# Fused attention and MLP on one core: the packed values computed with e1 stationary in 128x32 tiles, divided at once, and turned by two transposes

## Chip, cores and metric

The kernel runs on one core of a Trainium2 chip. The metric is the time of one execution on the device in microseconds (us); the number given for a kernel is the median of its runs.

## The reference

For each of 8 batches and 8 heads there are queries, keys and values of 576 rows by 64 columns, and 32 packed queries `p`. The attention is done twice: `p` attends to the keys and values, which gives 32 packed rows per head, and then the queries attend to those packed rows. The heads side by side give 4608 tokens of 512 columns, which go through a two-layer MLP.

```python
p_packed = sm_attn(p, k, v)            # softmax(p k^T / 8) v : 32 x 64 per head
out = sm_attn(q, p_packed, p_packed)   # softmax(q p_packed^T / 8) p_packed : 576 x 64 per head
x = out.transpose(0, 2, 1, 3).reshape(8 * 576, 512)
h = x @ w_in                           # 512 -> 2048
g = s * relu(h) ** 2 + b
y = g @ w_out                          # 2048 -> 512
```

## The kernel before

**Layout.** A batch is worked on as a whole. Heads are numbered `head(a, g) = 2g + a`, with `a` in 0..1 and `g` in 0..3, so that 4 groups of 32 packed rows fill 128 partitions for each `a`. The 576 rows of keys and values are taken in `NC = 6` chunks of `R = 96`.

**Stages of a batch.** Each has a letter in the order of work.

- `Tk`, `Tq` (`on_pe`, batches 0 and 1) or `Dk`, `Dq` (`on_dma`, later ones) turn keys and queries; `L..` are loads on the POOL queue; `V` (`order_v`) copies the loaded values, `vn`, into `vr`, ordered by chunk and head.
- `F` (`first_scores`) makes the scores of `p` against the keys, for one `a` at a time, and ScalarE writes their exponentials to `e1` (named `e` in the profile): 96 partitions, and for each `a`, chunk `c` and `g` 32 columns.
- `P` (`packed`) makes the packed values without their division. The stationary operand is `vr` of two heads (96x128), the moving one is `e1` of both `a` (64 columns); 6 chunks are summed for each of 4 head pairs, half of the pairs in `P.0` and half in `P.1`. Six more matmuls for each half, with `e1` stationary and a column of ones (`ones1`) moving, give the sums of the softmax. So a batch has 24 matmuls of 64 columns and 12 of one column in `pps`. The reciprocals of the sums go to `rd`, and with the scale to `rs`. The packed values are copied, undivided, to `ppd`, once in place and once to the other 64 partitions (`(c2, d)` on partitions, since the second scores want them in both halves): VectorE and ScalarE do two copies each.
- `S` (`second_scores`) makes the scores of the queries against `ppd` in 64x32 tiles of the array; their exponentials, with `rs` as a scale by pointer for each partition, are `e2` (also `e` in the profile). `A` (`weights`, for batch 0 `weights_half`) sums them with a block matrix of ones and divides: `aT`.
- `W` (`packed_w`) multiplies `ppd` by `w_in`, two chunks of 512 columns at a time, in 64x32 tiles; `scaled` copies the result to `pw` with `rd` as a scale, one half on ScalarE and one on VectorE.
- `M` (`mlp_in`, for batch 0 partly `mlp_in_half`, `h`) multiplies `pw` by `aT`: 4 matmuls of 288 columns into `hps`, a relu to `rlu`, a square to `gT`.
- `O` (`Out.step`) is the second layer: `Ob.txn` is `n` of the 16 matmuls of 512 columns that a block `t` of 128 tokens needs in `yps`; behind the sixteenth, VectorE writes `ysb` with the bias and the SP queue stores it.

`BT` (`bias_sums`) and `BC` (`bias_rows`) work out the bias once, from all of `w_out`, in batch 1's part; `BT` uses 128x32 tiles. `Z` and `Y` are matmuls of zeros that keep TensorE busy in the first microseconds.

**Order.** Nothing is scheduled at run time. Every instruction is pinned to the program's order on its engine (the helpers on lines 62, 65 and 73, which is why nearly all rows of the profile carry those lines), and the program's order is a list of words written out by hand:

```python
        O1.0x4 O1.1x2 P2.0 O1.1x1 P2.1 O1.1x5 W2.0 O1.1x6 S2 O1.1x2 O1.2x3 A2.0 O1.2x2 A2.1 O1.2x9 V3
```

So the `O` matmuls of one batch are the filling between the steps of the next one's attention, and the number behind an `x` is the time, in matmuls, that a step's followers have.

**PSUM.** `psh` has two buffers of two banks each, for all that is called `hps`; `psy` has four of one bank, for `yps`, `pps` and the like. The raw loads `kn`, `qn`, `vn` have one buffer each, and so have `vr`, `e1` and `e2`; `ppd`, `kT` and `qT` have two, by the batch's parity.

Of the kernel before, what the change touches and what calls it, by code (L numbers as in the profile page):

```python
# [14 lines left out]
def kernel(  # L15
# [18 lines left out]
    P = 128  # L34
# [68 lines left out]
    ones1 = constp.tile([P, 1], BF16, name="ones1")  # L103
# [45 lines left out]
    vr, e1, e2, rd, rs, aT, pw, pps, s2 = {}, {}, {}, {}, {}, {}, {}, {}, {}  # L149
# [38 lines left out]
    def on_pe(b, what, half):  # L188
# [5 lines left out]
        split = b == 0 and what == "q" and half == 1  # L194
# [24 lines left out]
    def order_v(b, h0=0, h1=H):  # L219
        if h0 == 0:  # L220
            vr[b] = attp.tile([R, NC, H, D], BF16, tag="vr", name="vr")
        vec.tensor_copy(
            out=vr[b][:, :, h0:h1, :].rearrange("r c h d -> r h c d"),
            in_=raw["v", b][:, h0:h1, :].rearrange("r h (c d) -> r h c d", c=NC),
        )
# [25 lines left out]
    def packed(b, half):  # L251

        if half == 0 or b == 0:
            pps[b] = psy.tile([P, NB], F32, tag="y", name="pps")
        pp = pps[b]
        for hp in range(2 * half, 2 * half + 2):
            for c in range(NC):
                mm(
                    pp[:, hp * 2 * NP:(hp + 1) * 2 * NP],
                    vr[b][:, c, 2 * hp:2 * hp + 2, :],  # L260
                    e1[b][:, :, c, hp, :],
                    start=(c == 0),
                    stop=(c == NC - 1),
                )
        a = half
        sums = pp[:, HP * 2 * NP:HP * 2 * NP + 2]
        for c in range(NC):
            mm(
                sums[:, a:a + 1],
                e1[b][:, a, c, :, :],  # L270
                ones1[0:R, :],
                start=(c == 0),
                stop=(c == NC - 1),
            )
        pd = ppd[b % 2]
        src = pp[:, 0:HP * 2 * NP].rearrange("p (g a j) -> p a g j", g=HP, a=2)
        if half == 0:
            rd[b] = smp.tile([P, 2], F32, tag="rd", name="rd")
            rs[b] = smp.tile([P, 2], F32, tag="rs", name="rs")
        if b == 0:  # L280
            vec.reciprocal(out=rd[b][:, a:a + 1], in_=sums[:, a:a + 1])
            gs = slice(2 * half, 2 * half + 2)
            for a in range(2):
                for to in (D * a, D - D * a):
                    (act.copy if half else vec.tensor_copy)(
                        out=pd[to:to + D, a, gs], in_=src[D * a:D * a + D, a, gs]
                    )
        elif half == 0:
            return
        else:  # L290
            vec.reciprocal(out=rd[b][:], in_=sums)
            for a in range(2):
                vec.tensor_copy(out=pd[D * a:D * a + D, a], in_=src[D * a:D * a + D, a])
                act.copy(out=pd[D - D * a:2 * D - D * a, a], in_=src[D * a:D * a + D, a])
        if half == 1:
            vec.tensor_scalar_mul(out=rs[b][:], in0=rd[b][:], scalar1=scale)

    def second_scores(b, by_half=False, with_w=False):
# [21 lines left out]
        for a in range(2):  # L320
            act.activation(
                out=e2[b][:, a, :].rearrange("p (i s) -> p i s", i=2),
                in_=tiles[a][:, :, 0:HS],
                func=AF.Exp,
                scale=rs[b][:, a:a + 1],
            )

    def exp_half(b, tiles, a, hf):
# [4 lines left out]
            scale=rs[b][:, a:a + 1],  # L333
        )

    def weights_half(b, hf):
# [3 lines left out]
        cols = slice(hf * HS, (hf + 1) * HS)  # L340
        for a in range(2):
            mm(dps[:, a, 0:HS], onesbd[:], e2[b][:, a, cols], start=True, stop=True)
        if hf == 0:
            exp_half(b, s2[b], 0, 1)
        ld = smp.tile([P, 2, HS], F32, tag="ld", name="ld")
        act.activation(out=ld[:], in_=dps[:, :, 0:HS], func=AF.Ln)
        rcd = smp.tile([P, 2, HS], F32, tag="rcd", name="rcd")
        act.activation(out=rcd[:], in_=ld[:], func=AF.Exp, scale=-1.0)
        if hf == 0:
            exp_half(b, s2[b], 1, 1)  # L350
        vec.tensor_tensor(out=aT[b][:, :, cols], in0=e2[b][:, :, cols], in1=rcd[:], op=ALU.mult)

    def weights(b, a):
# [7 lines left out]
        rcd = smp.tile([P, S], F32, tag="rcd", name="rcd")  # L361
        act.activation(out=rcd[:], in_=ld[:].rearrange("p a s -> p (a s)"), func=AF.Exp, scale=-1.0)
        vec.tensor_tensor(out=aT[b][:, a, :], in0=e2[b][:, a, :], in1=rcd[:], op=ALU.mult)

    def packed_w(b, chs):
# [20 lines left out]
        if len(chs) > 1:  # L386
            for a in range(2):
                dst = pw[b][:, a, chs[0] * NB:(chs[0] + 2) * NB].rearrange("p (i f) -> p i f", f=NB)
                scaled(b, a, dst, pair[a][:], a == 0)
        if len(chs) != 2:  # L390
            ch = chs[-1]
            for a in range(2):
                scaled(b, a, pw[b][:, a, ch * NB:(ch + 1) * NB], single[a][:], a == 0 and ch > 0)

    def scaled(b, a, out, in_, on_act):
        if on_act:
            act.activation(out=out, in_=in_, func=AF.Copy, scale=rd[b][:, a:a + 1])
        else:
            vec.tensor_scalar_mul(out=out, in0=in_, scalar1=rd[b][:, a:a + 1])
# [168 lines left out]
    def run(word):  # L568
# [35 lines left out]
        elif what == "P":  # L604
            packed(*n)
# [41 lines left out]
    vec.memset(ones1[:], 1.0)  # L647
# [69 lines left out]
```

## Time and profile before

| | |
|---|---|
| median of 3 runs | 253.81 us (253.78 to 254.29) |
| the profiled execution | 253.64 us, of which its span is 251.9 us |
| granted TensorE clock | 1.00 |
| TensorE busy | 243.2 us, 97% of the span |
| VectorE, ScalarE busy | 145.1 and 145.7 us, 58% each |
| largest groups on TensorE | 592 `yps` matmuls, 145.2 us; 512 `hps<-aT,pw`, 75.4 us |
| loads and stores | 35.48 MB in DMA packets, mean 141 GB/s |

The span runs from the first to the last instruction that the profiler saw on the core; the time of an execution is a little longer. A listed matmul length is the latency of one; matmuls overlap, so a group's busy time is less than count times length. A line of the timeline gives the start of a group, the time from its first start to its last end, its engine, its operands (out<-in), its tile (rows*columns of the array) and shape, its count, and in brackets the idle time of the engine before it and what ended it. `PEld` is the loading of stationary operands, which overlaps the matmuls.

### The profile page before, as it was taken

What the parts mean: (1) busy time and instruction counts of PE and PEld (TensorE: products, weight loads), DVE (VectorE), ACT (ScalarE), POOL (GpSimd) and SP (SyncE); (2) the same over time, 40 slices, a digit from 0 to 9 for tenths busy, and PEclk for the clock granted to TensorE, in tenths of its full rate; (3) what the DMA queues carried; (4) which work ended last, traced back from release to release, by engine and by line L of the source; (5) the groups of instructions that cost most, each with busy time, mean ns of one, the idle gap of its engine ahead of it and who ended that gap; (6) DMA issues with size and microseconds to landing.
All of it is one profiled execution on the core that took longest, in us unless ns stands there. A gap on an engine that the chain in (4) does not pass through costs nothing.

```text
span 251.9 us, 5279 instructions
## 1 busy us (share of the span) xinstructions
PE 243.2 (97%) x2178; PEld 136.8 (54%) x2178; DVE 145.1 (58%) x279; ACT 145.7 (58%) x235; POOL 29.1 (12%) x43
## 2 busy tenths in 40 slices
PE   7988899999999999999999999999999999999994
PEld 2554466356644664466546664466545665456553
DVE  4438767598547664476358544756364662664531
ACT  2357654668756854868387565567336785465400
POOL 8633212000300030000300030003000000000000
PEclk9999999999999999999999999999999999999999
DMA  6999999999795969439694979587987711120042
GB/s 73 179 206 207 203 203 200 201 193 185 131 221 126 180 110 214 96 83 186 113 216 86 187 128 217 108 158 132 216 176 138 140 37 46 52 75 1 3 125 85
DMA packets 59449, 35.48 MB, mean 141 GB/s; under 512 B 32160, under 2 KB 54944, under 8 KB 59424
## 3 DMA queue, kind: packets, MB, share of 16 engines
q0 software_dynamic: 25184, 18.61, 49.7%
q1 hardware_dynamic: 34192, 16.49, 29.4%
q8 instruction: 17, 0.28, 0.4%
q14 instruction: 8, 0.07, 0.1%
q10 hardware_dynamic: 48, 0.03, 0.0%
HBM read 37.23 MB, written 9.44 MB: 185 GB/s over the span
## 4 chain that ended last, share of the span: by engine, by line
PE 86%; DMA 10%; POOL 1%; issue 1%; DVE 0%; ACT 0%; POOLq 0%
PE yps L62 50%; PE hps L62 32%; DMA w_out_sb<-in_moe_w_out_dram 7%; DMA vn<-in_v_dram 3%; PE pps L62 3%; PE hps L65 1%; POOL kn L73 1%; POOL pn L73 0%; PE pps L65 0%; POOL vn L73 0%; DVE ysb L73 0%; ACT pbd L73 0%; POOL identb L73 0%; POOLq L73 0%; POOLq L701 0%
## 5 line engine op out<-in xcount | busy, mean ns | idle before, releaser
L62 PE MATMUL yps<-w_out_sb,gT 128*128 128x512 bf16 (+1 forms) x592 | 145.2, 374 | 0.7 <-DMA w_out_sb<-in_moe_w_out_dram 0.7
L73 ACT ACTIVATE rlu<-hps 128x576 bf16<-128x576 f32 x124 | 74.9, 648 | 35.2 <-PE hps L62 34.9
L62 PEld LDWEIGHTS <-gT 128*128 128x128 bf16 x592 | 54.6, 98 | 50.9 <-issue 7.4
L73 DVE TENSOR_TENSOR gT<-rlu 128x576 bf16<-128x576 bf16 x128 | 58.1, 458 | 33.1 <-ACT rlu L73 28.7
L62 PE MATMUL hps<-aT,pw 128*128 128x288 bf16 x512 | 75.4, 285 | 0.9 <-DVE pw L73 0.9
L62 PEld LDWEIGHTS <-pw 128*128 128x128 bf16 x512 | 49.5, 97 | 28.0 <-DVE pw L73 1.5
L73 DVE SCALAR_TENSOR_TENSOR ysb<-yps,svec,biasrep 128x512 f32<-128x512 f32 (+1 forms) x37 | 27.0, 733 | 21.6 <-PE yps L62 21.6
L73 DVE TENSOR_TENSOR aT<-e,rcd 128x576 bf16<-128x576 bf16 x16 | 12.1, 757 | 21.6 <-ACT rcd L73 21.5
L73 POOL DMA_DIRECT2D kn<-in_k_dram x9 | 6.9, 768 | 130.4 <-DMA kT<-kn 99.2
L73 ACT ACTIVATE pw<-hps,rd 128x1024 bf16<-128x1024 f32 x14 | 15.6, 1114 | 10.6 <-PE hps L62 10.4
L73 DVE TENSOR_SCALAR pw<-hps,rd 128x1024 bf16<-128x1024 f32 x14 | 17.9, 1280 | 3.9 <-PE hps L62 3.8
L73 ACT ACTIVATE e<-hps 96x768 bf16<-96x768 f32 x16 | 12.1, 803 | 8.2 <-PE hps L62 8.2
L73 ACT ACTIVATE e<-hps,rs 128x576 bf16<-128x576 f32 (+1 forms) x18 | 11.4, 684 | 6.4 <-PE hps L62 6.3
L73 ACT CAST ppd<-pps 64x128 bf16<-64x128 f32 (+1 forms) x18 | 4.5, 248 | 18.1 <-DVE ppd L73 16.1
L62 PE MATMUL zps<-zb 128*128 128x512 bf16 x42 | 12.1, 424 | 1.2 <-DVE zb L73 1.2
L73 ACT ACTIVATE ld<-hps 128x576 f32<-128x576 f32 x16 | 10.3, 645 | 3.2 <-PE hps L62 2.5
L62 PEld LDWEIGHTS <-ppd 64*32 64x32 bf16 x384 | 5.0, 89 | 11.7 <-issue 10.2
L73 ACT ACTIVATE rcd<-ld 128x576 f32<-128x576 f32 x16 | 10.9, 683 | 0.5
L62 PE MATMUL hps<-w_in_sb,ppd 64*32 64x512 bf16 x224 | 9.8, 381 | 0.0
L62 PEld LDWEIGHTS <-vr 96*128 96x128 bf16 x192 | 7.6, 97 | 3.2 <-issue 1.4
L73 DVE COPY vr<-vn 96x3072 bf16<-96x3072 bf16 (+1 forms) x9 | 7.7, 861 | 1.3 <-DMA vn<-in_v_dram 1.2
L62 PE MATMUL pps<-e,vr 96*128 96x64 bf16 x192 | 8.2, 192 | 0.2 <-ACT e L73 0.2
(60 smaller groups left out, 115.4 us busy)
## 6 DMA issues: line engine op xcount, KB each, us to landing
out_dram<-ysb SPq DMA_DIRECT2D x23, 192.0 KB, 2.4
kn<-in_k_dram POOLq DMA_DIRECT2D x7, 576.0 KB, 7.2
qn<-in_q_dram POOLq DMA_DIRECT2D x7, 576.0 KB, 12.4
vn<-in_v_dram POOLq DMA_DIRECT2D x7, 576.0 KB, 9.8
out_dram<-ysb SPq DMA_DIRECT2D x24, 128.0 KB, 2.4
w_in_sb<-in_moe_w_in_dram POOLq DMA_DIRECT2D x4, 512.0 KB, 13.3
w_out_sb<-in_moe_w_out_dram POOLq DMA_DIRECT2D x4, 512.0 KB, 18.5
out_dram<-ysb SPq DMA_DIRECT2D x23, 64.0 KB, 2.1
```

What stands on the lines that cost most here:

```text
L62: return tc.keep_in_program_order(nc.tensor.matmul(*a, **kw))
L65: return tc.keep_in_program_order(nc.tensor.transpose(*a, **kw))
L73: return lambda *a, **kw: tc.keep_in_program_order(f(*a, **kw))
```

## The change

`packed` swaps the operands. `e1` of one `a`, one chunk and one `g` (96x32) is stationary, at column tile `g` of the array, and `vr` of that head with a column of ones behind it (65 columns) is moving. A batch has 48 such matmuls, four tiles in turn, all of `a = 0` first; partitions of `pps` are now `(g, j)`, and column 64 holds the softmax sum of each partition. `vr` becomes one fixed tile, 66 columns a head, whose last two are set to 1.0 once. Behind the matmuls, VectorE takes the reciprocal of the sums and writes the divided values, twice side by side, to `pk`. A new step `X` (`turned`) transposes `pk` in two 128x128 transposes into the other half of `pps`' bank, and one VectorE copy of 256 columns fills `ppd`. Since `ppd` is now divided, `rs` is gone (the scale of the second exponentials is a constant) and `scaled` becomes `evict`, a copy without a scale.

For batch 0, `P` stays in two halves. Both halves of its `q` are split between ScalarE and VectorE, its second exponentials are all issued ahead of the logarithm, the product for `aT` becomes a word of its own (`G`, `weigh_half`), and the first chunk of `pw` is copied on VectorE in two halves of 256 columns (`first_w`, the second one at the word `E`). The list of words is written anew, with one `P` for each batch from 1 on, an `X` some five `O` behind it, and `O`, `M` and `W` in other places. The loads keep their order on the POOL queue. On the SP queue two stores stand ahead of one pair of `Dq`, `Dk` in place of behind it. Behind `BT` there are 544 `O` matmuls in place of 545.

```diff
-    ones1 = constp.tile([P, 1], BF16, name="ones1")
+    DV = D + 2
+    vr = constp.tile([R, NC, H, DV], BF16, name="vr")
...
-        split = b == 0 and what == "q" and half == 1
+        split = b == 0 and what == "q"
...
     def order_v(b, h0=0, h1=H):
-        if h0 == 0:
-            vr[b] = attp.tile([R, NC, H, D], BF16, tag="vr", name="vr")
         vec.tensor_copy(
-            out=vr[b][:, :, h0:h1, :].rearrange("r c h d -> r h c d"),
+            out=vr[:, :, h0:h1, 0:D].rearrange("r c h d -> r h c d"),
             in_=raw["v", b][:, h0:h1, :].rearrange("r h (c d) -> r h c d", c=NC),
         )
 
...
-    def packed(b, half):
-
-        if half == 0 or b == 0:
+    def packed(b, half=None):
+
+        if not half:
             pps[b] = psy.tile([P, NB], F32, tag="y", name="pps")
-        pp = pps[b]
-        for hp in range(2 * half, 2 * half + 2):
+        pp = pps[b][:, 0:2 * DV].rearrange("p (a x) -> p a x", a=2)
+        for a in range(2):
             for c in range(NC):
-                mm(
-                    pp[:, hp * 2 * NP:(hp + 1) * 2 * NP],
-                    vr[b][:, c, 2 * hp:2 * hp + 2, :],
-                    e1[b][:, :, c, hp, :],
-                    start=(c == 0),
-                    stop=(c == NC - 1),
-                )
-        a = half
-        sums = pp[:, HP * 2 * NP:HP * 2 * NP + 2]
-        for c in range(NC):
-            mm(
-                sums[:, a:a + 1],
-                e1[b][:, a, c, :, :],
-                ones1[0:R, :],
-                start=(c == 0),
-                stop=(c == NC - 1),
+                for g in range(4) if half is None else (2 * half, 2 * half + 1):
+                    mm(
+                        pp[NP * g:NP * g + NP, a, 0:D + 1],
+                        e1[b][:, a, c, g, :],
+                        vr[:, c, head(a, g), 0:D + 1],
+                        start=(c == 0),
+                        stop=(c == NC - 1),
+                        tile_position=(0, NP * g),
+                    )
+        if half == 0:
+            return
+        rd = smp.tile([P, 2], F32, tag="rd", name="rd")
+        vec.reciprocal(out=rd[:], in_=pp[:, :, D])
+        pk[b] = smp.tile([P, 2, 2, D], BF16, tag="pk", name="pk")
+        for a in range(2):
+            vec.tensor_scalar_mul(
+                out=pk[b][:, a],
+                in0=pp[:, a, 0:D].unsqueeze(1).to_broadcast([P, 2, D]),
+                scalar1=rd[:, a:a + 1],
             )
-        pd = ppd[b % 2]
-        src = pp[:, 0:HP * 2 * NP].rearrange("p (g a j) -> p a g j", g=HP, a=2)
-        if half == 0:
-            rd[b] = smp.tile([P, 2], F32, tag="rd", name="rd")
-            rs[b] = smp.tile([P, 2], F32, tag="rs", name="rs")
-        if b == 0:
-            vec.reciprocal(out=rd[b][:, a:a + 1], in_=sums[:, a:a + 1])
-            gs = slice(2 * half, 2 * half + 2)
-            for a in range(2):
-                for to in (D * a, D - D * a):
-                    (act.copy if half else vec.tensor_copy)(
-                        out=pd[to:to + D, a, gs], in_=src[D * a:D * a + D, a, gs]
-                    )
-        elif half == 0:
-            return
-        else:
-            vec.reciprocal(out=rd[b][:], in_=sums)
-            for a in range(2):
-                vec.tensor_copy(out=pd[D * a:D * a + D, a], in_=src[D * a:D * a + D, a])
-                act.copy(out=pd[D - D * a:2 * D - D * a, a], in_=src[D * a:D * a + D, a])
-        if half == 1:
-            vec.tensor_scalar_mul(out=rs[b][:], in0=rd[b][:], scalar1=scale)
+
+    def turned(b):
+
+        pt = pps[b][:, NB // 2:].bitcast(BF16)
+        for a in range(2):
+            tr(pt[:, a * P:(a + 1) * P], pk[b][:, a].rearrange("p c d -> p (c d)"), identb[:])
+        vec.tensor_copy(
+            out=ppd[b % 2][:].rearrange("p a g j -> p (a g j)"),
+            in_=pt[:, 0:2 * P],
+        )
 
...
-                scale=rs[b][:, a:a + 1],
+                scale=scale,
...
     def weights_half(b, hf):
         if hf == 0:
             aT[b] = atp.tile([P, 2, S], BF16, tag="aT", name="aT")
         dps = big()
-        cols = slice(hf * HS, (hf + 1) * HS)
         for a in range(2):
-            mm(dps[:, a, 0:HS], onesbd[:], e2[b][:, a, cols], start=True, stop=True)
+            mm(dps[:, a, 0:HS], onesbd[:], e2[b][:, a, hf * HS:(hf + 1) * HS], start=True, stop=True)
         if hf == 0:
             exp_half(b, s2[b], 0, 1)
+            exp_half(b, s2[b], 1, 1)
         ld = smp.tile([P, 2, HS], F32, tag="ld", name="ld")
         act.activation(out=ld[:], in_=dps[:, :, 0:HS], func=AF.Ln)
-        rcd = smp.tile([P, 2, HS], F32, tag="rcd", name="rcd")
-        act.activation(out=rcd[:], in_=ld[:], func=AF.Exp, scale=-1.0)
-        if hf == 0:
-            exp_half(b, s2[b], 1, 1)
-        vec.tensor_tensor(out=aT[b][:, :, cols], in0=e2[b][:, :, cols], in1=rcd[:], op=ALU.mult)
+        rcd[hf] = smp.tile([P, 2, HS], F32, tag="rcd", name="rcd")
+        act.activation(out=rcd[hf][:], in_=ld[:], func=AF.Exp, scale=-1.0)
+
+    def weigh_half(b, hf):
+        cols = slice(hf * HS, (hf + 1) * HS)
+        vec.tensor_tensor(out=aT[b][:, :, cols], in0=e2[b][:, :, cols], in1=rcd[hf][:], op=ALU.mult)
 
...
-                scaled(b, a, dst, pair[a][:], a == 0)
+                evict(dst, pair[a][:], a == 0)
         if len(chs) != 2:
             ch = chs[-1]
+            if ch == 0:
+                s2["w"] = single
+                first_w(b, 0)
+                return
             for a in range(2):
-                scaled(b, a, pw[b][:, a, ch * NB:(ch + 1) * NB], single[a][:], a == 0 and ch > 0)
-
-    def scaled(b, a, out, in_, on_act):
+                evict(pw[b][:, a, ch * NB:(ch + 1) * NB], single[a][:], a == 0)
+
+    def first_w(b, half):
+
+        cols = slice(2 * P * half, 2 * P * half + 2 * P)
+        for a in range(2):
+            vec.tensor_copy(out=pw[b][:, a, cols], in_=s2["w"][a][:, cols])
+
+    def evict(out, in_, on_act):
         if on_act:
-            act.activation(out=out, in_=in_, func=AF.Copy, scale=rd[b][:, a:a + 1])
+            act.copy(out=out, in_=in_)
         else:
-            vec.tensor_scalar_mul(out=out, in0=in_, scalar1=rd[b][:, a:a + 1])
+            vec.tensor_copy(out=out, in_=in_)
...
-            packed(*n)
+            packed(n[0], *(n[1:] if n[0] == 0 else ()))
+        elif what == "G":
+            weigh_half(*n)
+        elif what == "E":
+            first_w(0, 1)
+        elif what == "X":
+            turned(*n)
...
-    vec.memset(ones1[:], 1.0)
+    vec.memset(vr[:, :, :, D:DV], 1.0)
...
-        Lwi0 Lwi1 Lwi2 Lwi3 Lwo0 Lwo1 Lp1 Tk0.0 Z10 PD Tk0.1 Lk1 PP0 Z3 F0.0 V0.0 F0.1 V0.1 Z5 P0.0 P0.1
-        Tq0.0 Z3 Tq0.1 Lq1 Lv1 Lwo2 Lwo3 Lpall Z2 S0 Z3 A0.0 W0.0 Z3 A0.1 Z1 h0.0.0 h0.2.0 W0.1 Y1
-        h0.0.1 h0.2.1 W0.2 M0.4 M0.5 Y1 M0.6 W0.3 M0.7 O0.0x4 M0.8 M0.9 PD1 O0.0x2 M0.10 M0.11 O0.0x2
-        O0.1x2 PP1 M0.12 O0.1x1 Tk1.1 Tk1.0 Lk2 O0.1x3 M0.13 O0.1x1 F1.0 O0.1x1 Tq1.1 O0.2x1 Tq1.0
-        O0.2x1 F1.1 O0.2x1 V1 Lv2 Lq2 O0.2x1 M0.14 O0.2x1 M0.15 P1.0 O0.2x1 P1.1 O0.2x1 O0.0x4 S1 O0.1x4
-        BT PA A1.0 O0.0x3 BC A1.1 O0.1x3 O0.2x3 W1.0 O0.0x1 O0.1x1 O0.2x5 W1.2 V2 O0.2x1 O0.3x5 M1.0
-        O0.3x1 M1.1 O0.3x1 M1.2 Dq2 Dk2 Lk3 Lv3 Lq3 O0.3x1 M1.3 PPA M1.4 M1.5 O0.3x8 O1.0x1 M1.6 M1.7
-        O1.0x2 M1.8 M1.9 O1.0x2 M1.10 M1.11 O1.0x2 M1.12 M1.13 O1.0x2 M1.14 M1.15 O1.0x3 F2.0 F2.1
...
+        Lwi0 Lwi1 Lwi2 Lwi3 Lwo0 Lwo1 Lp1 Tk0.0 Z10 PD Tk0.1 Lk1 PP0 Z3 F0.0 V0.0 F0.1 Z5 P0.0 V0.1 P0.1
+        Z2 Tq0.0 Z1 X0 Z1 Tq0.1 Lq1 Lv1 Lwo2 Lwo3 Lpall Z4 S0 Z3 A0.0 W0.0 Z1 A0.1 G0.0 E Z1 h0.0.0 W0.1
+        G0.1 h0.2.0 Y2 h0.0.1 h0.2.1 W0.2 M0.4 W0.3 M0.5 M0.6 O0.0x1 M0.7 O0.0x3 M0.8 M0.9 O0.1x1 PD1
+        O0.0x1 M0.10 M0.11 O0.0x3 O0.1x1 PP1 M0.12 O0.1x2 Tk1.0 Tk1.1 Lk2 O0.1x2 M0.13 O0.1x1 F1.0
+        O0.1x1 Tq1.0 O0.2x1 Tq1.1 O0.2x1 F1.1 O0.2x2 V1 Lv2 Lq2 M0.14 P1.1 M0.15 O0.2x3 O0.0x2 X1 O0.0x2
+        O0.1x1 S1 O0.1x3 O0.2x1 BT PA A1.0 O0.0x3 BC A1.1 O0.1x3 O0.2x3 W1.0 O0.0x1 O0.1x1 O0.2x5 W1.2
+        V2 O0.3x6 M1.0 PPA M1.1 M1.2 Dq2 Dk2 Lk3 Lv3 Lq3 O0.3x9 M1.3 M1.4 O0.3x1 O1.0x1 M1.5 M1.6 O1.0x2
+        M1.7 M1.8 O1.0x2 M1.9 M1.10 O1.0x2 M1.11 M1.12 O1.0x2 M1.13 M1.14 O1.0x2 M1.15 O1.0x2 F2.0 F2.1
+        O1.0x3 O1.1x3 P2.1 O1.1x5 X2 O1.1x3 S2 O1.1x4 A2.0 O1.1x1 O1.2x1 A2.1 O1.2x7 W2.0 O1.2x8 O1.3x1
...
```

## The prediction, made before the changed kernel ran

> **What bounds the kernel now.** I read the page first: busy times and the chain that ended last.
>
> ```profile
> PE 243.2 (97%) x2178; PEld 136.8 (54%) x2178; DVE 145.1 (58%) x279; ACT 145.7 (58%) x235; POOL 29.1 (12%) x43
> ...
> PE 86%; DMA 10%; POOL 1%; issue 1%; DVE 0%; ACT 0%; POOLq 0%
> ...
> L62 PE MATMUL pps<-e,vr 96*128 96x64 bf16 x192 | 8.2, 192 | 0.2 <-ACT e L73 0.2
> ```
>
> TensorE is the bound, and VectorE and ScalarE, at 58% each, matter only where TensorE waits for them. The 10% of DMA lies at the start. The chain and the tile view of `w_out_sb` (its last load alone) show where it ends:
>
> ```profile
> 12.29 18.15 DMA w_out_sb<-in_moe_w_out_dram
> ...
> 30.48 0.59 PE yps L62 x2
> ```
>
> ```profile
> L73 POOL DMA_DIRECT2D w_out_sb<-in_moe_w_out_dram x1: 747/747/747, 25.5 to 25.5; - x1
> ...
> DMA to landing us min/median/max: 19.0/19.0/19.0
> ```
>
> The second chunk of `w_out` lands at 30.44 and TensorE starts on it at 30.48; the fourth lands at 25.5 + 19.0 = 44.5, and the sums for the bias (`BT`), which read all four chunks, start at 44.56. So the order of time has a pin at 44.5. The queue of loads is the same in both kernels. What is saved ahead of the pin is lost in it; what is saved behind it counts in full, because from 44.5 to 206.5 TensorE is busy in every stretch that the table of windows gives.
>
> Next the timeline around one packed step, batch 3 (start, length, engine):
>
> ```profile
> 94.40 1.50 ACT L73 ACTIVATE e<-hps 96x768 bf16<-96x768 f32 x2 [1.86 <-PE hps L62]
> ...
> 94.55 1.46 PE L62 MATMUL yps<-w_out_sb,gT 128*128 128x512 bf16 x6
> 95.96 0.51 PE L62 MATMUL pps<-e,vr 96*128 96x64 bf16 x12
> 96.31 0.29 PE L62 MATMUL pps<-ones,e 96*128 96x1 bf16 x6
> 96.46 0.51 PE L62 MATMUL pps<-e,vr 96*128 96x64 bf16 x12
> 96.81 0.29 PE L62 MATMUL pps<-ones,e 96*128 96x1 bf16 x6
> 96.96 1.24 PE L62 MATMUL yps<-w_out_sb,gT 128*128 128x512 bf16 x5
> ```
>
> A matmul's listed length (192 ns) is latency; what it costs the stream is the distance of starts. 24 of 64 columns and 12 of one column go from 95.96 to 96.96: **1.00 us**, 29 ns and 25 ns each. Ahead of them, the sixth `yps` starts at 94.55 + 1.46 - 0.38 = 95.63 and streams 0.216, to 95.85; the first `pps` starts 0.11 later, just after ScalarE's second exponential ends (94.40 + 1.50 = 95.90), because its moving `e1` spans both values of `a`. The same 0.11 stands before batches 2 to 5.
>
> Last, the only place where the old kernel uses 128x32 tiles, the bias sums, and a burst of tiled weight loads:
>
> ```profile
> 43.82 0.81 PE L62 MATMUL yps<-w_out_sb,gT 128*128 128x512 bf16 x3
> ...
> 44.56 1.05 PE L62 MATMUL hps<-w_out_sb,onesb 128*32 128x512 bf16 x16
> 45.54 0.42 PE L62 MATMUL hps<-e,onesbd 128*128 128x288 bf16 x2
> ...
> 49.00 0.14 PEld L62 LDWEIGHTS <-ppd 64*32 64x32 bf16 x16 [0.42 <-issue]
> ```
>
> Sixteen matmuls of 512 columns have their last start 1.05 - 0.38 = 0.67 after the first. That is three rounds of 0.22: **four column tiles stream at once**, each from its own rows of `w_out_sb`, and the next round's weights load under the running one. Entering costs 44.56 - (43.82 + 3 x 0.216) = 0.09, and leaving 45.54 - (45.23 + 0.216) = 0.09. The 16 loads of the last line (89 ns latency each) start within 0.05 us: instructions in the queue go out every 3 to 4 ns.
>
> **What the Trainium skill says.** "TensorE: Matmul & The Clock Gate", Part 3 (The mechanism): tiles at different positions overlap, about 4 ns between starts; the bias sums agree. The same page, Back-to-back issue gap: N/2.4 + 2.5 ns and a floor near 25 ns; the trace has 29 ns at 64 columns and 25 at one. "TensorEngine Tiling (Array Packing)", Key Properties: a change of tiling mode drains the array; the trace has 0.09 in and 0.09 out. Its Restrictions say that column tiling gives up fast weight load; the trace shows no exposed load in the bias sums, but there each had 0.21 us to hide in.
>
> **The change on TensorE, for a batch behind the pin (2 to 7).**
> - Removed: 1.00 us of `pps` stream.
> - Added: 48 matmuls of 65 columns, in rounds of four tiles. That is 12 rounds of 65/2.4 + 2.5 = 29.6 ns, 0.36 us, plus 0.185 to enter and leave the mode. Bounds of a round: 27 ns (the stream alone) and 42 ns, if the load does not hide (tiled matmuls of `S`, 64x32, list 279 to 294 ns, so a load in the open is worth up to 15), which is 0.33 to 0.51 us. I take 0.36, since the bias sums hide their loads.
> - Added: two transposes of 128 columns (`X`). The pair in `prep_p` has starts 0.06 apart, with no gap to its neighbours, so 0.11 us. Sum: 1.00 - 0.36 - 0.185 - 0.11 = 0.34 us saved, 2.06 us in six batches.
> - The wait for the second exponential goes: the new loop does all of `a = 0` first, so `a = 1` is wanted about 0.27 us later (mode entry and six rounds), past the 0.11. Four times 0.11 = 0.44 us. What is late next is nothing: in batches 6 and 7 there was no such wait already.
> - One `O` matmul moves from behind `BT` to ahead of it (544 against 545 behind): 0.22 us.
>
> **The new wait, X.** Behind `P` stand `reciprocal` (0.17), two products (128 columns; rows of 745 ns at 512 and 1280 at 1024 give 1.045 ns a column and 0.21 fixed, so 0.34; a second in a row 0.08 less) and two handovers to semaphores of about 0.05. With 0.19 for the last matmul's latency, `pk` is ready about 1.1 us after that matmul starts. `X` comes after five `O`: 0.03 + 0.09 + 5 x 0.216 = 1.2 us. It fits by 0.1 if VectorE is free; the order has it free at that point in all six. Bounds: no wait, to 0.15 us a batch (0.9 in all); I take 0.1 in all. Behind `X` a copy of 256 columns (rows of 753 ns at 1152 and 458 at 576 give 0.29) is due three to five `O` later (0.65 to 1.1 us). In batches 3, 5 and 7 a `ysb` (0.75) is ahead of it on VectorE, and there the distance is four or five `O`. I count nothing. Stuck behind a late `X` would be TensorE's whole stream, and behind that `W`, `S` and the `ppd` readers.
>
> **Edits at no cost.** VectorE loses two casts and `rs` a batch (0.28 + 0.26 + 0.17), gains 0.60 + 0.29; both ScalarE casts (0.26 each) go, and its scales by pointer. Neither engine ends a wait there; their cover is TensorE's 97%. The copy into `vr` (0.95) keeps runs of 64 values, now 66 apart; if it took twice as long, it would still lie in stretches where VectorE is idle 40% of the time (15.9 us busy of 27.0 from 94 to 121). The memset of the ones runs while the first load is awaited (VectorE idles 2.3 us for `kT`). Batch 0's regrouped evictions, `G`, `E` and the split of `qT`, and batch 1's `P1`/`X1`, lie ahead of the pin; TensorE has 0.7 us to spare at 30.48. Worked through from `vn1` (landing 39.28, copy to 40.26): `P1` starts at 40.3, then 0.36 + 0.09, `M0.15` 0.49, twelve `O` 2.59, `X1` 0.11 and `S1` 0.46, which is 44.4 against 44.5. `BT` may slip by up to 0.3 if `X1` waits; that is in the range. The moved store ahead of `Dq`/`Dk` on SP, in one batch, delays two transposes that are wanted over 10 us later. POOL's order is the same.
>
> **Sum.** 2.06 + 0.44 + 0.22 - 0.1 = 2.6 us. The profiled execution is 253.64 (span 251.9 and 1.7 around it), 0.2 under the median of 253.81. So 251.0 against its own time, and **251.2** as the median.
>
> **Rivals.**
> - *Instructions do not come fast enough (slower).* 48 pairs in 0.36 us is 7.5 ns a pair. The trace shows 3 to 4 ns only for 16 pairs that were queued; the fastest long run is 25 ns. The skill gives TensorE a queue of 64 ("Advanced Engine Details and Errata", Engine Queue Depths), 32 pairs; estimated from it and 25 ns a pair, the other 16 take 0.4, which costs 0.07 a batch. But if the rate of 25 ns held for all 48, or the tiles of 96 rows ran one after another (that the change doesn't do what it says), `P` would take 1.2 us, a batch would cost 1.2 + 0.185 + 0.11 against 1.00 + 0.07, and the time would be 253.8 + 6 x 0.42 - 0.2 = **256.1**. It decides from 17 ns a pair on. For it: no long burst is seen. Against it: 16 of 16 went at full rate each time.
> - *X is late.* If VectorE holds another piece (0.46 for a `gT`, 0.75 for a `ysb`) between `P` and `pk`, 0.4 to 0.6 us a batch: 6 x 0.35 net leaves **253.2**. Against it: the order on VectorE puts `rd` and `pk` ahead of both.
> - *More than that.* The waits of `S7` (0.23 for ScalarE's `ppd`), `F7` (0.17) and two of 0.08 also go: **250.6**.
>
> **Chances.** As worked out 0.68 (its own range 250.7 to 252.7); more 0.08; late X or slow rounds 0.09 (252.7 to 253.5); starved or serial tiles 0.12; no change by other losses 0.03. A measurement can tell about 0.2% (0.5 us) from no change. Faster by more than that 0.80, within 0.05, slower 0.15. The range 250.4 to 253.1 leaves out the serial case and the ends.
>
> **What would show it.** Right: `pps` in 128x32 form with 48 starts within 0.36 to 0.45 us; 0.09 before and after; no idle of TensorE at the transposes; `BT` again at about 44.6; the rest shorter by 2.6. Wrong: starts of `pps` 17 ns or more apart on average, TensorE idle before `pt` with VectorE `pk` as releaser, or `BT` later than 45.

## The result and the profile after

The changed kernel takes **249.84 us** (median of 4 runs, 249.40 to 250.21), against 253.80 in the same measurement: a ratio of 0.984, 95% interval 0.982 to 0.986. It is faster by 1.6%, which is 4.0 us, where 2.6 were forecast and the range ended at 3.4. The profiled execution took 250.06 us, its span is 248.3 us. The experiments ran on other chips, where the first keys land 1.5 us later (7.4 in place of 5.9). In some executions there TensorE works at half rate for some microseconds more at the start, which lengthens them by 1 to 2.6 us, and "at full clock" means the others. The yardstick across runs is the stretch from the start of `BT` to the start of the last matmul, which is the same to 0.02 us in both traces of the changed kernel.

From the page and its chain of waits, the lines that answer to those of before:

```profile
PE 239.0 (96%) x2291; PEld 132.2 (53%) x2291; DVE 144.5 (58%) x278; ACT 138.9 (56%) x218; POOL 29.1 (12%) x43
...
PE 82%; DMA 16%; issue 1%; POOL 0%; DVE 0%; POOLq 0%
...
22.81 19.49 DMA w_out_sb<-in_moe_w_out_dram
```

TensorE is still the bound. The DMA share of the chain has grown from 10% to 16%, because the chain now leaves TensorE for the third chunk of `w_out`, which lands at 22.81 + 19.49 = 42.30. The timeline of batch 3 after, to be read beside the one of before:

```profile
96.56 0.56 PE L62 MATMUL pps<-vr,e 96*32 96x65 bf16 x48
...
97.05 1.25 PE L62 MATMUL yps<-w_out_sb,gT 128*128 128x512 bf16 x5
97.19 0.17 DVE L73 RECIPROCAL rd<-pps 128x2 f32<-128x2 f32 x1 [3.06 <-PE pps L62]
97.40 0.61 DVE L73 TENSOR_SCALAR pk<-pps,rd 128x128 bf16<-128x128 f32 x2
...
98.14 0.28 PE L65 MATMUL pps<-identb,pk 128*128 128x128 bf16 x2
...
98.79 0.28 DVE L73 COPY ppd<-pps 128x256 bf16<-128x256 bf16 x1
...
99.42 0.63 PE L62 MATMUL hps<-w_in_sb,ppd 64*32 64x512 bf16 x16
```

The 48 matmuls start within 0.56 - 0.20 = 0.36 us (0.20 is the latency of the last), and the next `yps` starts at 97.05. `pk` is ready at 97.40 + 0.61 = 98.01, and `X` comes at 98.14 with no idle time in brackets. So in this batch the step itself did what was forecast.

Where the time went shows in the starts of the single matmuls, summed from `BT` to the last matmul: 203.59 us before, 199.62 after, 3.97 less.

| | forecast | measured |
|---|---|---|
| `P` without its entries, `X`, entries and exits of the tiled mode | -2.06 | -1.87 |
| wait for the second exponential | -0.44 | -0.44 |
| one `O` fewer behind `BT` | -0.22 | -0.22 |
| wait before `X` (batch 6 alone) | +0.1 | +0.04 |
| inside the calls of `W` | 0 | **-1.04** |
| inside the calls of `S` | 0 | **-0.35** |
| rest | 0 | -0.09 |

`BT` itself starts 0.40 later (44.97 for 44.56), so the profiled execution is 3.6 us shorter, and not 3.97. The missed 1.4 us stand in two rows of the groups by line that I had not set beside each other. Before:

```profile
L62 PE MATMUL hps<-w_in_sb,ppd 64*32 64x512 bf16 x224 | 9.8, 381 | 0.0
...
L62 PE MATMUL hps<-qT,ppd 64*32 64x288 bf16 x128 | 4.2, 289 | 0.1
```

After:

```profile
L62 PE MATMUL hps<-w_in_sb,ppd 64*32 64x512 bf16 x224 | 8.8, 381 | 0.0
...
L62 PE MATMUL hps<-qT,ppd 64*32 64x288 bf16 x128 | 3.5, 288 | 0.0
```

Count, shape and mean latency are the same, the idle time is nil in both, and yet the busy time of `W` is 1.0 us less. With tiled matmuls several are in flight, and TensorE counts as busy while one of them runs; a wait of the next one within the same call is then no idle time, but a longer group. The timeline of before, batch 3, has such calls:

```profile
97.86 0.29 DVE L73 CAST ppd<-pps 64x128 bf16<-64x128 f32 x1 [0.38 <-ACT ppd L73]
98.13 0.22 PEld L62 LDWEIGHTS <-ppd 64*32 64x32 bf16 x16 [0.42 <-issue]
98.13 0.70 PE L62 MATMUL hps<-w_in_sb,ppd 64*32 64x512 bf16 x16
...
98.93 1.28 DVE L73 TENSOR_SCALAR pw<-hps,rd 128x1024 bf16<-128x1024 f32 x1 [0.57 <-PE hps L62]
...
100.16 0.72 PE L62 MATMUL hps<-w_in_sb,ppd 64*32 64x512 bf16 x16
```

The call of 99.42 above, without a wait, has 0.63, and its sixteen loads take 0.14 where these take 0.22. In `W3.0` the second matmul starts 82 ns after the first instead of 3, beside the end of VectorE's second cast to `ppd` (98.15). In `W3.2` it is 102 ns, beside the end of VectorE's `pw` of the call before (100.21), which frees the second of the two `hps` buffers. A call of `W` without a wait takes 0.56 us from its first start to the next instruction; over the fourteen calls behind `BT`, 1.08 us are above that: 0.62 for `ppd` (five calls), 0.38 for `pw` (four calls, batch 1 among them) and 0.09 in `W5.2`, beside the end of ScalarE's `ld`, which reads an `hps` buffer too. The changed kernel keeps 0.04 of it, in `W3.2`. In `S7` the ninth matmul waits 0.24 for ScalarE's last cast to `ppd`, in `S4` 0.09 for `pw`.

### The profile page after: what moved, and what is told of

The parts are those of the page before. It is cut to its first block, busy times and chain, and to the rows that moved or that the text cites. A ratio compares the mean times of both kernels' runs of the same rounds, so it can differ in the third digit from the quotient of the medians.

```text
span 248.3 us, 5498 instructions
## 1 busy us (share of the span) xinstructions
PE 239.0 (96%) x2291; PEld 132.2 (53%) x2291; DVE 144.5 (58%) x278; ACT 138.9 (56%) x218; POOL 29.1 (12%) x43
## 4 chain that ended last, share of the span: by engine, by line
PE 82%; DMA 16%; issue 1%; POOL 0%; DVE 0%; POOLq 0%
PE yps L62 49%; PE hps L62 30%; DMA w_out_sb<-in_moe_w_out_dram 8%; DMA w_in_sb<-in_moe_w_in_dram 5%; DMA kn<-in_k_dram 2%; PE pps L62 1%; PE pps L65 1%; POOL kn L73 0%; DVE ysb L73 0%; POOL identb L73 0%; POOLq L73 0%; POOLq L707 0%
## 5 line engine op out<-in xcount | busy, mean ns | idle before, releaser
L62 PE MATMUL hps<-aT,pw 128*128 128x288 bf16 x512 | 76.4, 285 | 2.3 <-DVE aT L73 2.3
L73 ACT ACTIVATE e<-hps 96x768 bf16<-96x768 f32 (+2 forms) x34 | 21.8, 693 | 30.4 <-PE hps L62 30.3
L73 ACT CAST pw<-hps 128x1024 bf16<-128x1024 f32 x14 | 14.2, 1012 | 16.5 <-PE hps L62 15.7
L73 DVE CAST pw<-hps 128x1024 bf16<-128x1024 f32 x14 | 17.1, 1218 | 2.7 <-PE hps L62 2.7
L62 PEld LDWEIGHTS <-ppd 64*32 64x32 bf16 x384 | 3.5, 88 | 10.3 <-issue 6.9
L62 PE MATMUL hps<-w_in_sb,ppd 64*32 64x512 bf16 x224 | 8.8, 381 | 0.0
L62 PEld LDWEIGHTS <-kT 128*128 128x128 bf16 x192 | 6.9, 98 | 2.4 <-issue 0.6
L73 DVE RECIPROCAL rd<-pps 128x2 f32<-128x2 f32 x8 | 1.4, 170 | 11.3 <-PE pps L62 11.3
L62 PEld LDWEIGHTS <-zb 128*128 128x128 bf16 x45 | 4.4, 108 | 6.2 <-issue 2.9
L73 POOL DMA_DIRECT2D vn<-in_v_dram x9 | 6.7, 751 | 6.2 <-DVE vr L73 4.5
```

The lines of the kernel that those rows point to most:

```text
L62: return tc.keep_in_program_order(nc.tensor.matmul(*a, **kw))
L73: return lambda *a, **kw: tc.keep_in_program_order(f(*a, **kw))
```

## The experiments

My theory after the result: these waits went because the new list of words puts the steps further apart. Before, five `O` (four in batch 5) lay between `P` and the first reader of `ppd`, and mostly six between two calls of `W` or `W` and `S`; now it is eight to ten from `P`, and in batches 2 and 4 to 7 nine to thirteen between the calls (batch 3 still has six, batch 1 seven as before). The rival: they went because the steps' chains are shorter (ScalarE's casts and the pointer scales are gone). A second question is what sets the start of `BT`.

| kernel | median us | ratio to before (95%) | at full clock | `BT` to last matmul |
|---|---|---|---|---|
| e5, changed | 250.31 | 0.982 (0.980 to 0.984) | 250.2 to 250.5 | 199.64 |
| e1, old steps, new order | 253.44 | 0.995 (0.993 to 0.997) | 252.9 to 253.5 | 202.24 |
| e2, new steps, old order | 251.76 | 0.988 (0.985 to 0.991) | 251.5 to 251.8 | 200.78 |
| e3, half of late `w_out` | 250.99 | 0.984 (0.981 to 0.987) | 250.2 to 250.5 | 199.64 |
| e4, batch 0 as before | 251.99 | 0.987 (0.984 to 0.989) | 251.1 | 199.65 |
| e6, tiles in turn | 252.93 | 0.992 (0.990 to 0.995) | 252.7 to 253.1 | 201.73 |
| e7, `X` two earlier | 252.77 | 0.992 (0.990 to 0.994) | 252.4 to 253.2 | 201.82 |
| e8, `S` with the first `W` | **249.22** | 0.978 (0.976 to 0.980) | 249.1 to 249.7 | 198.47 |
| e9, `M0.15` ahead of `P1` | 250.63 | 0.983 (0.977 to 0.988) | 250.4 to 250.7 | 199.65 |
| e10, e9 and e3 | 250.50 | 0.982 (0.977 to 0.987) | 250.4 to 250.6 | 199.66 |
| e11, e4 again | 251.60 | 0.985 (0.981 to 0.989) | 250.8 to 251.2 | 199.65 |
| e12, e8 and e9, `BT` later | 251.44 | 0.983 (0.979 to 0.988) | 250.3 to 250.4 | 198.41 |

The kernel before took 254.8, 254.7 and 254.8 us beside e1 to e4, e5 to e8 and e9 to e12. In the table e12's stretch is not comparable, since its `BT` stands elsewhere.

**e1: the order alone.**

The steps are those of the kernel before; the list behind `BT` is the changed one for every batch, as here for batch 2, with one `O` more ahead of `W1.2`.

```diff
-        O1.0x4 O1.1x2 P2.0 O1.1x1 P2.1 O1.1x5 W2.0 O1.1x6 S2 O1.1x2 O1.2x3 A2.0 O1.2x2 A2.1 O1.2x9 V3
-        O1.2x2 W2.2
+        O1.0x3 O1.1x3 P2.0 P2.1 O1.1x5 O1.1x3 S2 O1.1x4 A2.0 O1.1x1 O1.2x1 A2.1 O1.2x7 W2.0 O1.2x8 O1.3x1
+        V3 O1.3x1 W2.2
```

> The steps of the kernel before, with the changed kernel's order of words behind BT (X dropped, P.0 and P.1 together where P stands). Theory 'distance': the 1.4 us that I had not forecast are waits inside W and S (the second matmul of W.0 on VectorE's ppd, the first matmuls of W.2 on VectorE's pw of the W before), and they go because the words stand further apart: then they go here too, with P's 1.00 us a batch left as it was, and the time is 253.8 - 1.0 (W) - 0.35 (S) = 252.4 us, 252.0 to 252.8. Rival 'shorter chains': they go because ScalarE's ppd casts and the pointer scale are gone: then they stay here and the time is 253.8, 253.5 to 254.0.

Measured: 1.35 us less from `BT` to the last matmul, 1.4 us at full clock. In the single starts, the waits inside `W` fall from 1.08 to 0.10 us (`W3.2` alone keeps one) and those inside `S` from 0.35 to nothing, with ScalarE's casts and pointer scales in place. So distance is enough to remove them, and the rival falls: it wanted the time of the kernel before.

**e2: the steps alone.**

The steps are those of the changed kernel, the list behind `BT` that of the kernel before but for `P`, `X` and one `O` less ahead of `W1.0`. With `X` five `O` behind `P` and the first reader of `ppd` three behind `X`, that reader stands eight `O` behind `P`, where the kernel before has four or five.

```diff
-        O1.0x3 O1.1x3 P2.1 O1.1x5 X2 O1.1x3 S2 O1.1x4 A2.0 O1.1x1 O1.2x1 A2.1 O1.2x7 W2.0 O1.2x8 O1.3x1
-        V3 O1.3x1 W2.2
+        O1.0x4 O1.1x2 P2.1 O1.1x5 X2 O1.1x3 W2.0 O1.1x6 S2 O1.2x5 A2.0 O1.2x2 A2.1 O1.2x7 V3 O1.2x2 W2.2
```

> The changed kernel's steps, with the order of the kernel before behind BT as far as it can be kept: one P, X five O behind it, the first reader of ppd three O behind X, W.2 or S six O behind W.0. Theory 'distance': the forecast's 2.6 us alone are gained, 251.2 us (250.9 to 251.5), and the table of W shows its second pair of chunks waiting for VectorE's pw by 0.05 to 0.15 in batches 3, 5, 6, 7. Rival 'shorter chains': as the changed kernel, 249.8 (249.5 to 250.2). In between, if the new steps take away the waits on ppd and the order those on pw: 250.4 to 250.8.

Measured: 2.80 us less than before from `BT` on, 3.1 us at full clock, 1.2 to 1.3 short of the changed kernel. It is the case in between: the first calls of `W` in batches 2 to 7 have no wait inside, the second ones of batches 3, 5, 6 and 7 still do, by 0.25 in all, and batch 1's two by 0.20: together 0.45 us where the changed kernel has 0.04. Of the other 0.75, some 0.5 are single waits elsewhere in this order (0.18 before an `M`, 0.17 at `F7`, 0.14 for `ppd` before `W4.0`, 0.11 at two `X`, less what the changed kernel has of such); some 0.2 I have not assigned. So of the 0.47 us of waits in `W` for `pw` and `ld`, 0.37 stay with the new steps in the old order: these went by distance in the main. The shorter eviction helps a little: `W3.2` stands six `O` behind `W3.0` in all four kernels and waits 0.10 with the old steps (before, e1) and 0.04 with the new ones (changed, e2), where VectorE's `pw` takes 1.22 us in place of 1.28. Whether the shorter chain alone would have removed the waits for `ppd` (0.62) e2 does not show, since its readers stand further from `P` as well.

**e5: the changed kernel once more**, as the yardstick.

> The changed kernel unaltered, as the yardstick of this group of runs and of the one before, since the kernel before took 254.7 us on the chip of that one in place of 253.8. Behind BT it should again take 199.6 us to the last matmul. If batch 0's regrouping is lost ahead of the pin, it is no faster than e4 (3.6 us under the kernel before in runs at full clock); if the regrouping counts, 3.9 to 4.3 us under the kernel before.

Measured: 199.64 from `BT` to the last matmul (199.62 in the first trace), 4.3 us under the kernel before.

**e6: no four tiles at once.**

```diff
-            for c in range(NC):
-                for g in range(4) if half is None else (2 * half, 2 * half + 1):
+            for g in range(4) if half is None else (2 * half, 2 * half + 1):
+                for c in range(NC):
                     mm(
```

> The changed kernel with the loops over g and c exchanged, so that all six chunks of one column tile stand one behind the other and the next tile follows only then. Theory 'four tiles at once' (a round of four costs one stream, 29.6 ns): without it the 48 matmuls cost 25 to 30 ns each, P takes 1.2 to 1.45 us in place of 0.36, and the time is 6 x (0.85 to 1.1) = 5 to 6.5 us longer behind BT, 255 to 256.5: slower than the kernel before, the rival's 256.1. Rival 'the rate comes from instructions alone, at 7.4 ns a pair whatever the tile': P stays at 0.36 to 0.45 us and the time within 0.5 us of the changed kernel's.

The timeline of this kernel's batch 3:

```profile
98.81 0.91 PE L62 MATMUL pps<-vr,e 96*32 96x65 bf16 x48
99.65 0.82 PE L62 MATMUL yps<-w_out_sb,gT 128*128 128x512 bf16 x3
```

Measured: the starts spread over 0.91 - 0.19 = 0.72 us, twice the 0.36 of the interleaved loop, and the stretch is 2.1 us longer. So the order of the tiles matters, but a matmul costs 15.3 ns and not 25 to 30: both theories miss. The starts are uneven, 0 to 38 ns apart, with a pattern that repeats every 80 ns, six starts at a time; how TensorE overlaps these tiles no run here settles. The prediction's slower rival priced tiles in turn at 25 ns and gave 256.1; with the measured price it is 249.8 + 2.1 = 252, under the kernel before. The overlap of tiles at different positions, which the prediction took from the Trainium skill, "TensorE: Matmul & The Clock Gate", Part 3 (The mechanism), is stronger here than I made of it.

**e7: X closer to P.**

In batches 2 to 7, as here:

```diff
-        O1.0x3 O1.1x3 P2.1 O1.1x5 X2 O1.1x3 S2
+        O1.0x3 O1.1x3 P2.1 O1.1x3 X2 O1.1x5 S2
```

> The changed kernel with X three O behind P in place of five in batches 2 to 7 (two O moved from ahead of X to behind it). By the prediction's working, pk is ready 1.1 us after the start of the last P matmul (measured since: 1.09), and X would come at 0.03 + 0.09 + 3 x 0.216 = 0.77: TensorE waits 0.33 us in each of six batches, 2.0 us in all, with DVE's pk as releaser. Rival 'the distance has slack' (pk's products overlap with more than the trace shows): under 0.5 us longer.

From the waits of TensorE:

```profile
PE pps L65 <- DVE pk L73: 1.3, 6, 0.3
```

Measured: six waits, and in the starts each `X` comes 0.35 us late, that of batch 6 0.49 (the view's 1.3 counts only time in which nothing is in flight); 2.18 us longer from `BT` on, 2.4 at full clock. The handover of 1.1 us and its place are as the prediction worked them out: five `O` are just enough, with 0.08 to spare in five batches and 0.04 too little in batch 6.

**e3, e9, e10: what sets the start of BT.**

In e3 and e10 `d1` is 256 for the last two chunks of `w_out` and the other columns are set to zeros, which leaves that part of the output out; in e9 and e10 the words change.

```diff
-            out=w_out_sb[:, m0:m1, :],
-            in_=moe_w_out[m0 * P:m1 * P, :].rearrange("(m p) d -> p m d", p=P),
+            out=w_out_sb[:, m0:m1, 0:d1],
+            in_=moe_w_out[m0 * P:m1 * P, 0:d1].rearrange("(m p) d -> p m d", p=P),
...
-        V1 Lv2 Lq2 M0.14 P1.1 M0.15 O0.2x3 O0.0x2 X1
+        V1 Lv2 Lq2 M0.14 M0.15 P1.1 O0.2x3 O0.0x2 X1
```

> The changed kernel, but of the third and fourth chunk of w_out only the first 256 columns are loaded, the others are zeros (that part of the output is left out). Theory 'pin': the start of BT is set by loads; TensorE waits 0.56 us for the third chunk at 41.6 and BT reads the fourth, so BT starts 0.5 us earlier (44.4 in place of 44.97) and the time is 249.3, 249.0 to 249.5. If the wait for vr (0.79 at 39.2) also shrinks because the loads ahead of it are shorter, down to 248.7. Rival 'no pin': batch 0 and 1 are bound by their own chains, BT stays within 0.1 and the time at 249.8.

> The changed kernel with M0.15 ahead of P1 in place of behind it, so that its 0.49 us of TensorE time lies in the wait of 0.7 to 0.8 us for vr that stands before P1. Theory 'two loads set BT': the start of BT is the later of two chains, vn of batch 1 (landing, copy, P1 and 4.2 us of work) and the third chunk of w_out (landing and 2.6 us of work); in the runs so far both ended within 0.6 us of each other. Then only the first gets shorter, and 0 to 0.2 us is gained. Rival 'vn alone': 0.5 us is gained, 249.8 on the chip of e5 (250.3).

> e9's order, and of the third and fourth chunk of w_out the first 256 columns alone are loaded (the output's other part is left out), so that both chains get shorter. Theory 'two loads set BT': now the time falls by about 0.5 us against the changed kernel, though e3, with the loads halved alone, gained nothing (250.44 against 250.31 at full clock) and e9 alone gains little: BT 0.5 us earlier. Rival 'batch 0's own work sets BT': no gain here either.

Measured: none of them gains (250.2 to 250.7 at full clock, as e5), so "pin" in e3, "vn alone" in e9 and "two loads" in e10 are refuted in the form that I gave them. Why shows in the timeline of e10 between the landing of `vn` (39.79) and `BT`:

```profile
39.82 0.96 DVE L73 COPY vr<-vn 96x3072 bf16<-96x3072 bf16 x1 [0.21 <-DMA vn<-in_v_dram]
...
40.69 0.75 DVE L73 TENSOR_SCALAR rlu<-hps 128x576 bf16<-128x576 f32 x1
...
41.47 0.83 DVE L73 TENSOR_TENSOR gT<-rlu 128x576 bf16<-128x576 bf16 x2
...
42.22 0.16 DVE L73 RECIPROCAL rd<-pps 128x2 f32<-128x2 f32 x1
42.42 0.61 DVE L73 TENSOR_SCALAR pk<-pps,rd 128x128 bf16<-128x128 f32 x2
...
43.08 0.27 PE L65 MATMUL pps<-identb,pk 128*128 128x128 bf16 x2 [0.42 <-DVE pk L73]
```

From the landing of `vn` on VectorE works without a gap (copy, `M0.14`'s relu, two `gT`, `rd`, `pk`), and `X1` waits for its end. In the changed kernel's own order (e5) the same queue ends 0.2 us ahead of `X1`, and TensorE has no gap from `P1` to `BT`. So filling TensorE's wait before `P1` only moves the wait to `X1`. From the landing of `vn` to `BT` it is 5.29 us in e5 and e11 and 5.48 in e10; in the first trace of the changed kernel, in e7 and in e8 it is 5.85, 5.89 and 5.78, of which a wait for the third chunk of `w_out` makes 0.56, 0.60 and 0.49. So `BT` follows the load of batch 1's values and the work behind it on VectorE and TensorE; the third chunk adds up to 0.6 in some executions, and the fourth, which I had named, binds nothing here. This is read from the timelines: no run moves the landing of `vn` alone. It also holds only at full clock. In the trace of e3 `vn` lands at 40.06, but VectorE still has batch 1's queries:

```profile
39.69 1.49 DVE L73 COPY qT<-hps 128x1152 bf16<-128x1152 bf16 x2 [0.27 <-PE hps L65]
41.09 0.95 DVE L73 COPY vr<-vn 96x3072 bf16<-96x3072 bf16 x1
```

There the work ahead of the load does set `BT` (46.35), about 1 us later.

**e4, e11: batch 0's regrouping undone.**

```diff
-        split = b == 0 and what == "q"
+        split = b == 0 and what == "q" and half == 1
...
-            exp_half(b, s2[b], 1, 1)
...
+        if hf == 0:
+            exp_half(b, s2[b], 1, 1)
+        else:
+            weigh_half(b, 1)
...
-                first_w(b, 0)
+                weigh_half(b, 0)
+                for a in range(2):
+                    vec.tensor_copy(out=pw[b][:, a, 0:NB], in_=single[a][:])
```

The early words are in their old order too, without `G` and `E`.

> The changed kernel with batch 0's regrouping undone: the first half of q turned on one engine, the last exponentials behind the first logarithm, the product for aT where it was, the first chunk of pw copied whole, the early words in their old order. Theory 'pin': what this saves or costs lies ahead of the loads of w_out and vn of batch 1 and is lost there: 249.8, within 0.2. Rival 'batch 0 counts': BT comes later by what the regrouping saves, 0.3 to 1.0 us, and the time is 250.1 to 250.8.

> e4 once more, since it came out 0.8 us above e5 at full clock, where I had counted nothing, and 0.53 us of it lay behind the last matmul of its trace, in the landing of the last store (3.25 us after that matmul's start in place of 2.72). If that landing is a matter of this program and not of chance, it is there again; up to the last matmul I expect the time of e5 within 0.3 us. Rival 'batch 0 counts': BT later than e5's by 0.5 us or more at full clock, with the store as in the others.

Start of the bias sums, first in e5, then in e11:

```profile
45.13 1.05 PE L62 MATMUL hps<-w_out_sb,onesb 128*32 128x512 bf16 x16
```

```profile
45.13 1.05 PE L62 MATMUL hps<-w_out_sb,onesb 128*32 128x512 bf16 x16
```

Measured: `BT` at the same hundredth, and the same stretch behind it. Up to the last matmul the regrouping is worth nothing, as forecast. Of the 0.6 to 0.8 us more that e4 and e11 take, 0.53 and 0.57 lie behind the last matmul: the last store lands 3.25 and 3.29 us after that matmul's start, in all other kernels here 2.71 to 2.73. What in this program does that stays open.

**e8: one stay in the tiled mode less.** The first 512 columns of `W` go out with `S`, into two banks of `psy`; the other three chunks at the later place of `W`.

```diff
-            packed_w(b, [0])
+            wps = packed_w(b, [0])
...
+        if with_w:
+            for a in range(2):
+                evict(pw[b][:, a, 0:NB], wps[a][:], a == 0)
...
-            second_scores(n[0], by_half=n[0] == 0)
+            second_scores(n[0], by_half=n[0] == 0, with_w=n[0] > 1)
...
-            packed_w(n[0], [n[1], n[1] + 1] if n[0] else [n[1]])
+            packed_w(n[0], [1, 2, 3] if n[0] > 1 else [n[1], n[1] + 1] if n[0] else [n[1]])
...
-        A2.1 O1.2x7 W2.0 O1.2x8 O1.3x1 V3 O1.3x1 W2.2
+        A2.1 O1.2x15 O1.3x1 V3 O1.3x1 W2.2
```

> The changed kernel with one stay in the tiled mode less in batches 2 to 7: the first 512 columns of W go out with S, into two banks of psy, and the other three chunks at the later one of W's two places. If a stay costs 0.093 in and 0.092 out wherever it lies, 6 x 0.185 = 1.1 us is saved: 248.7 against 249.8 for the changed kernel. Rival 'new waits': two banks of psy held longer, or three chunks evicted at once (1.2 us for each half) stop M or the next yps, and half or more of it is lost: 249.3 or above.

Its timeline in batch 3:

```profile
102.57 0.44 PE L62 MATMUL hps<-qT,ppd 64*32 64x288 bf16 x16
102.83 0.40 PE L62 MATMUL wps<-w_in_sb,ppd 64*32 64x512 bf16 x8
103.16 1.04 PE L62 MATMUL yps<-w_out_sb,gT 128*128 128x512 bf16 x4
```

Measured: the eight of `W` follow the sixteen of `S` with no change of mode between them, and the stretch is 1.17 us shorter, for 6 x 0.185 = 1.11 expected. At 249.22 us it beats the changed kernel beside it (250.31) by 1.1 us and the kernel before by 5.4.

**e12: joined.**

```diff
-        X1 O0.0x2 O0.1x1 S1 O0.1x3 O0.2x1 BT PA A1.0 O0.0x3 BC A1.1 O0.1x3 O0.2x3 W1.0
+        X1 O0.0x2 O0.1x1 S1 O0.1x3 O0.2x1 PA A1.0 O0.0x3 BT A1.1 O0.1x3 O0.2x3 BC W1.0
```

> e8 (S and the first chunk of W in one stay in the tiled mode) with M0.15 ahead of P1 and BT, BC three and six O later, where the fourth chunk of w_out has landed in any case. Theory 'two loads set BT': 0 to 0.2 us under e8, 249.0 to 249.2. Rival 'BT's place counts': the matmuls behind BT no longer wait for it and 0.4 us is gained, 248.8.

```profile
50.09 1.02 PE L62 MATMUL hps<-biasrep,rowsf 128*128 128x512 f32 x2
51.04 0.39 PE L62 MATMUL hps<-w_in_sb,ppd 64*32 64x512 bf16 x1
51.95 0.62 PE L62 MATMUL hps<-w_in_sb,ppd 64*32 64x512 bf16 x15 [0.53 <-DVE biasrep L73]
```

Measured: 250.3 to 250.4 at full clock, 1.1 worse than e8 (the kernel before took 254.6 at full clock beside both). With `BC` right ahead of `W1.0`, the second buffer of `hps` is still `BC`'s, and `W1.0` stands from 51.04 to 51.95 until VectorE has read it: 0.9 of the 1.1. Neither theory had that.

## Why the prediction was wrong in size and right in kind

- **The P stream** was forecast at 0.36 us of starts and 0.09 in and out; measured 0.36, 0.09 and 0.10. With `X` the six batches gave 1.87 for 2.06: before, `P` cost 1.005 a batch, after 0.693 for the 0.66 of the sum. Right.
- **The second exponential** (0.44) and **the moved O** (0.22): as forecast. Batch 1's `P1` at 40.15, forecast 40.3.
- **The new wait, X**: forecast 1.1 against 1.2 us, measured 1.09 against 1.22, no wait, in five batches; e7 shows the price if it is two `O` closer. Right; of the 0.1 that I took off, 0.04 came, in batch 6, where VectorE, though idle, starts the reciprocal 0.12 later than in the others; why stays open.
- **The step that failed is a term that the sum puts at nothing**: what the casts and the new order of words do to the waits inside `W` and `S`. Of VectorE and ScalarE the prediction says "Neither engine ends a wait there", and for the order it counts one moved `O`. Measured: 1.04 us inside `W` and 0.35 inside `S`, together 1.39 of the 3.97. The rival "more than that" (0.56 us, 0.08 of the chances) held only waits that a view shows as idle time. Its wait of `S7` did go, and with that of `S4` this makes the 0.35; its `F7` wait went but 0.12 came back at `F2`; not in it at all were the 1.04 us inside `W`. I had read the zero in the idle column of that row as no wait. The trace of before had the number: a call without a wait costs 0.56 us to the next instruction, fourteen calls 7.8, and the group took 8.89. e1 shows that the new order alone is worth 1.35 us, e2 that the new steps with little of the new order give 2.8, near the 2.6 that I had summed.
- **The pin** held as a fact at full clock (`BT` at 44.97 for 44.56, and nothing gained ahead of it counts: e9, e10, e11), but its cause was misnamed: not the fourth chunk of `w_out`, but `vn` of batch 1 and the work behind it, with the third chunk at times. That the fourth chunk lands just ahead of `BT` is a coincidence, and the prediction's own sum had the sign: between the last `O` and `BT` it found 0.09, the price of entering the mode, which leaves no wait for a load. From the landing of `vn` to `BT` it is 5.28 us in the kernel before too.
- **Edits at no cost**: batch 0's regrouping is worth nothing up to the last matmul (e11). The casts into `ppd` that left ScalarE and VectorE had been on the path, in the `ppd` waits of `W`.
- **The slower rival** (25 ns a pair) did not come, and e6 shows that even tiles in turn cost 15.3 ns, under the 17 from which it would have decided.

## What to carry to other kernels

Compare the busy time of a group with count times the spacing of a call that has no wait: with tiled matmuls a wait inside a call is not idle time, and only the sum of starts shows it. When a diff rewrites an order written by hand, measure for each step the distance to its first reader in instructions of the filling, before and after, since here these distances were worth half as much as the new instructions themselves (1.35 us against 2.6). And count the stays in a tiled mode: each costs about 0.19 us here whether 16 matmuls are done in it or 48, so work that shares a mode should share a stay.

## What the hardware showed that I had not expected

- Six matmuls on one column tile, then six on the next, still run at 15.3 ns each (e6), half of the 29 ns that one stream needs; so these tiles overlap without being interleaved, though only half as well as with four in turn (7.6 ns).
- 48 pairs of load and matmul in a row came at 7.6 ns each without starving; the longest such burst in the trace before had 16.
- A stay in the tiled mode costs 0.09 in and 0.09 to 0.10 out, for 16 matmuls of `W` or `S` as for 48 of `P`: e8 saved 1.17 us by six stays less. The Trainium skill, "TensorEngine Tiling (Array Packing)", Key Properties, says that a change of tiling mode drains the array and gives no figure; that these times are the drain is the natural reading, which no run here tests.
